# Moving one batch's v casts from GpSimd to VectorE, and working that batch's q halves in a row

## The chip, the cores and the metric

The kernel runs on one core of a Trainium2 chip. The metric is the device time of one execution in microseconds (us). A core has five engines with a queue each, worked in order: TensorE (PE in the profile, its weight loads PEld), VectorE (DVE), ScalarE (ACT), GpSimd (POOL) and SyncE (SP), which here only issues DMA transfers. Engines wait for each other through semaphores.

## The reference

Eight batches of linear attention feed a feed-forward layer with a "snake" activation:

```python
q_s = exp(q - max(q)) / sum(exp(q - max(q)))      # over the head dimension
k_s = exp(k - max(k)) / sum(exp(k - max(k)))      # over the sequence
kv  = einsum('bhsd,bhse->bhde', k_s, v)
a   = einsum('bhsd,bhde->bhse', q_s, kv)          # batch, heads, 576 rows, 64
x   = a.transpose(0, 2, 1, 3).reshape(4608, 512)
h   = x @ w_in                                    # 512 -> 2048
g   = h + sin(alpha * h)**2 / (alpha + 1e-9)
out = g @ w_out                                   # 2048 -> 512
```

q, k and v are float32 of shape (8, 8, 576, 64). The matmuls run in bfloat16.

## The kernel before

The 4608 rows are cut into nine tiles of 512. For a tile t, TensorE makes 16 blocks `hp` of 128 x 512 (four matmuls each). ScalarE takes the sine, one of three engines the square, VectorE combines `hp` and the square into `g`, and the second layer's matmuls (`op`) of tile t run under tile t + 1. A batch has 576 rows, so attention for the next batch is worked inside the tiles: batch 3 in tile 2. For it the kernel needs, on the way into tile 2, `qn` (q, exponential taken, divided by its sum, in two halves) and `vb` (v cast to bfloat16).

```python
def cast_v(b, engs):
    vv = vb[b % 2].rearrange("p j (i c) -> p i j c", i=4)
    for ii in range(2):                              # two casts of 128 x 1152
        engs[ii](vv[:, 2 * ii:2 * ii + 2, :, 0:D], staged["v", b][:, ii::2])

def norm_q(b, engs, j1=J, between=None):
    ...
    for ii in range(2):                              # two multiplies of 128 x 1152
        part = qs[:, 0:j1, 2 * ii:2 * ii + 2]
        if ii == 1 and between:
            between()
        ...
        engs[ii % len(engs)].tensor_tensor(qn[:, ii, 0:j1]..., qe[:, ii], part..., op=ALU.mult)
```

The head of tile 2, with cuts:

```python
kv_norm(2)
norm_q(3, [GP], between=lambda: cast_v(3, [GP_CP, GP_CP]))
take(os, 20)                                  # output matmuls of tile 1
...                                           # attention output of batch 2 into xT: tile 2's input
take(os)
q_transpose_dma(3)                            # on SyncE, waits for both halves of qn
load_batch(4)                                 # behind it in SyncE's queue
...
SQ2 = "PAPPAPAPPAPAPPAP"                      # who squares: P GpSimd, A ScalarE
for ni in range(nN):
    h_slot(2, ni, SQ2[ni], lag, lent)         # hp block, sine, square
    flush(lag, 2)                             # combine, two blocks behind
    attn_back(3, ni - 5, (DVE_CP, ACT_CP), (5, 7, 9, 10))
```

`attn_back` puts batch 3's key-value matmuls (`kvp`, 36 small ones) behind hp block 5, and its four output pairs (`xp`, one PSUM buffer) behind blocks 10, 12, 14 and 15. PSUM is the memory that TensorE accumulates into; from `kvp` VectorE makes `kbd`, which the `xp` matmuls take. There are four `hp` buffers in PSUM, plus two lent ones for blocks 4, 5, 10 and 11 (they bear the name `op` in the profile), and four `s` tiles for the sines. So block 6 can't start until combine 0 has freed a buffer.

The softmax here doesn't subtract the row's maximum and nothing guards it: scores larger than these inputs give would overflow.

## Time and profile before

| | before |
|---|---|
| median time (range, the first three runs) | 290.53 us (290.14 to 291.12) |
| profiled span | 288.3 us |
| TensorE busy, granted clock | 272.6 us (95%), 1.00 |
| GpSimd busy | 81.9 us (28%) |
| TensorE idle from 80 to 100 us | 2.75 us |

The page draws each engine's busy time in 40 slices of 7.2 us, a digit being tenths, 9 meaning 90% or more. TensorE's row of the kernel before:

```profile
PE   2899999999978999999999999999999999999994
```

Between the start and the end, the only digits under 9 are the 7 and the 8 in slices 12 and 13, at 79 to 94 us. This is tile 2's head, and the rest of the reading of before is in the prediction below.

### The profile page before, as it was taken

How to read it: one execution, taken by the hardware profiler on the slowest of the kernel's cores; microseconds unless marked ns; L12 is line 12 of the kernel's file. 1: busy time of each engine (PE TensorE's matmuls, PEld its weight loads, DVE VectorE, ACT ScalarE, POOL GpSimd, SP SyncE). 2: the span in 40 equal slices, each digit the busy share in tenths (PEclk: the TensorE clock that was granted, in tenths of full speed). 3: DMA queues.
4: the chain of work that ended last, by engine and by line, in shares of the span. 5: the costliest groups of instructions: out<-in, count | busy, mean ns of one | idle time of the engine just before them, and what ended most of it. 6: DMA issues, size and time to landing. Idle time of an engine off the chain costs nothing.

```text
span 288.3 us, 4247 instructions
## 1 busy us (share of the span) xinstructions
PE 272.6 (95%) x1541; PEld 130.7 (45%) x1569; DVE 189.4 (66%) x289; ACT 225.9 (78%) x321; POOL 81.9 (28%) x77
## 2 busy tenths in 40 slices
PE   2899999999978999999999999999999999999994
PEld 1444454445444445444544454445444444444443
DVE  4867967999839567856776677757674555555422
ACT  4898648999449999899889988999877777777400
POOL 2969502772486662005300440032000000000000
PEclk9999999999999999999999999999999999999999
DMA  7999999843959957119911990115011111111242
GB/s 263 305 201 243 258 399 407 298 163 89 273 121 374 411 208 140 38 38 356 291 24 24 330 343 3 38 39 132 22 39 36 36 36 39 36 38 38 46 101 73
DMA packets 38581, 45.77 MB, mean 159 GB/s; under 512 B 16528, under 2 KB 22432, under 8 KB 38560
## 3 DMA queue, kind: packets, MB, share of 16 engines
q1 hardware_dynamic: 33376, 40.57, 45.0%
q0 software_dynamic: 4992, 4.79, 9.6%
q8 instruction: 12, 0.20, 0.3%
q10 hardware_dynamic: 192, 0.14, 0.2%
q14 instruction: 9, 0.07, 0.1%
HBM read 36.71 MB, written 9.44 MB: 160 GB/s over the span
## 4 chain that ended last, share of the span: by engine, by line
PE 78%; DVE 6%; DMA 5%; POOL 4%; ACT 4%; issue 2%; ACTq 0%
PE op L270 37%; PE hp L250 33%; DMA st_v<-in_v_dram 3%; ACT s L256 3%; POOL s L260 2%; DVE g L266 2%; PE kvp L173 2%; PE xp L222 2%; DMA st_q<-in_q_dram 1%; PE op L590 1%; PE hh L250 1%; DVE qn L154 1%; DVE qs L152 1%; POOL vb L137 1%; POOL qn L154 1%
## 5 line engine op out<-in xcount | busy, mean ns | idle before, releaser
L266 DVE SCALAR_TENSOR_TENSOR g<-s,inva_sb,hp 128x512 bf16<-128x512 f32 x130 | 96.1, 745 | 64.2 <-ACT s L258 54.2
L250 PE MATMUL hp<-xT,win 128*128 128x512 bf16 x512 | 128.9, 379 | 2.3 <-DVE g L266 1.7
L270 PE MATMUL op<-wout,g 128*128 128x512 bf16 x479 | 121.8, 379 | 1.2 <-issue 0.6
L256 ACT ACTIVATE s<-hp,alpha_sb 128x512 f32<-128x512 f32 x130 | 87.9, 683 | 25.1 <-PE hp L250 22.6
L250 PEld LDWEIGHTS <-win 128*128 128x128 bf16 x576 | 56.3, 98 | 69.6 <-issue 3.0
L270 PEld LDWEIGHTS <-g 128*128 128x128 bf16 x560 | 54.1, 98 | 61.1 <-issue 0.4
L258 ACT ACTIVATE s<-s 128x512 f32<-128x512 f32 x111 | 69.9, 630 | 3.6
L154 POOL TENSOR_TENSOR qn<-qe,qs 128x1152 bf16<-128x1152 bf16 (+1 forms) x12 | 24.9, 2093 | 78.7 <-DVE qs L146 69.4
L260 POOL TENSOR_TENSOR s<-s 128x512 f32<-128x512 f32 x30 | 32.0, 1079 | 22.5 <-ACT s L256 22.2
L276 DVE COPY o<-op 128x512 f32<-128x512 f32 (+2 forms) x33 | 22.1, 669 | 9.7 <-PE op L270 5.8
L118 ACT ACTIVATE ke<-st_k 128x1152 bf16<-128x1152 f32 x16 | 17.9, 1151 | 5.1 <-DMA st_k<-in_k_dram 5.1
L118 ACT ACTIVATE qe<-st_q 128x1152 bf16<-128x1152 f32 (+3 forms) x18 | 17.6, 1024 | 2.1 <-DMA st_q<-in_q_dram 1.9
L145 DVE TENSOR_REDUCE qs<-qe 128x36 f32<-128x2304 bf16 x5 | 12.8, 2553 | 8.7 <-ACT qe L118 8.6
L137 POOL CAST vb<-st_v 128x1152 bf16<-128x1152 f32 x12 | 13.6, 1164 | 7.6 <-DMA st_v<-in_v_dram 6.4
L270 PE MATMUL hp<-wout,g 128*128 128x512 bf16 x62 | 14.8, 379 | 0.2 <-issue 0.2
L225 DVE CAST xT<-xp 128x512 bf16<-128x512 f32 (+1 forms) x18 | 13.4, 743 | 0.0
L173 PE MATMUL kvp<-vb,ke 64*128 64x130 bf16 x288 | 9.9, 216 | 0.8 <-ACT vb L137 0.4
L173 PEld LDWEIGHTS <-ke 64*128 64x128 bf16 x288 | 8.4, 93 | 5.0 <-issue 2.5
L118 ACT ACT_TABLE_LOAD x7 | 9.0, 1283 | 1.3 <-PEq L604 1.2
L250 PE MATMUL hh<-xT,win 128*128 128x512 bf16 x39 | 9.6, 379 | 0.1
L222 PE MATMUL xp<-qT,kbd 128*128 128x256 bf16 (+1 forms) x40 | 8.2, 286 | 0.8 <-DVE xT L225 0.8
L152 DVE TENSOR_REDUCE qs<-qe 128x16 f32<-128x1024 bf16 (+2 forms) x6 | 7.2, 1198 | 1.9 <-ACT qe L118 1.9
(79 smaller groups left out, 119.5 us busy)
## 6 DMA issues: line engine op xcount, KB each, us to landing
out_dram<-o SPq DMA_DIRECT2D x70, 128.0 KB, 2.3
st_q<-in_q_dram SPq DMA_DIRECT2D x6, 1152.0 KB, 5.9
st_k<-in_k_dram SPq DMA_DIRECT2D x6, 1152.0 KB, 8.2
st_v<-in_v_dram SPq DMA_DIRECT2D x6, 1152.0 KB, 10.1
st_k<-in_k_dram SPq DMA_DIRECT2D x4, 576.0 KB, 7.1
wout<-in_moe_w_out_dram POOLq DMA_DIRECT2D x4, 512.0 KB, 11.7
st_v<-in_v_dram SPq DMA_DIRECT2D x3, 576.0 KB, 9.4
win<-in_moe_w_in_dram POOLq DMA_DIRECT2D x6, 256.0 KB, 7.6
```

What stands on the lines that cost most here:

```text
L118: nc.scalar.activation(dst[:, :, ii * 128:(ii + 1) * 128].rearrange("p j (x d) -> p x j d", x=2), src[:, ii::2], AX.Exp)
L137: engs[ii](vv[:, 2 * ii:2 * ii + 2, :, 0:D], staged["v", b][:, ii::2])
L154: engs[ii % len(engs)].tensor_tensor(qn[:, ii, 0:j1].rearrange("p j (x d) -> p j x d", x=2), qe[:, ii], part.unsqueeze(3).to_broadcast([12 ...
L173: nc.tensor.matmul(kvp[:, e, ii * 130:(ii + 1) * 130], ke[r, j, ii * 128:(ii + 1) * 128], vt[r, j, ii * 130:(ii + 1) * 130], start=(j == 0 ...
L222: nc.tensor.matmul(xp[:, e, 0:n], kt[:, e, ii], qT[:, ii, j0:j1, e * 64:(e + 1) * 64], start=True, stop=True)
L250: nc.tensor.matmul(hp, win[:, ki, ni * 128:(ni + 1) * 128], xT[:, ki, t * MF:(t + 1) * MF], start=(ki == 0), stop=(ki == 3))
L256: nc.scalar.activation(s, hp, AX.Sin, scale=alpha_sb[:, ni:ni + 1])
L258: nc.scalar.activation(s, s, AX.Square)
L260: nc.gpsimd.tensor_tensor(s, s, s, op=ALU.mult)
L266: nc.vector.scalar_tensor_tensor(G[t][:, ni], in0=s, scalar=inva_sb[:, ni:ni + 1], in1=hp, op0=ALU.mult, op1=ALU.add)
L270: nc.tensor.matmul(acc, G[t][:, ni, j * 128:(j + 1) * 128], wout[:, ni, :], start=(ni == 0), stop=(ni == nN - 1))
L276: eng(o[:, cols], acc)
```

## The change

Its intent is to take GpSimd's two casts of v, and their wait for the load of v, out of the way of the second half of q and of tile 2's first squares.

```diff
-    def norm_q(b, engs, j1=J, between=None):
+    def norm_q(b, engs, j1=J):
...
-            if ii == 1 and between:
-                between()
...
-    norm_q(3, [GP], between=lambda: cast_v(3, [GP_CP, GP_CP]))
+    norm_q(3, [GP])
     take(os, 20)
...
     take(os)
+    cast_v(3, [DVE_CP, DVE_CP])
     q_transpose_dma(3)
     load_batch(4)
```

## The prediction

> **What bounds the kernel now.** I read the page first, then the chain that ended last between 60 and 100 us, then the timelines of TensorE, GpSimd, VectorE, ScalarE and SyncE there, then the table of busy time in stretches of 10 us.
>
> ```profile
> PE 272.6 (95%) x1541; PEld 130.7 (45%) x1569; DVE 189.4 (66%) x289; ACT 225.9 (78%) x321; POOL 81.9 (28%) x77
> ```
>
> TensorE is busy for 272.6 of 288.3 us at a granted clock of 1.00 throughout. A change that touches no matmul can gain only idle TensorE time. The table shows 1.91 us of it in 80 to 90 us and 0.84 in 90 to 100, against 0.05 to 0.21 in the steady stretches behind. That is the head of tile 2, where the changed lines run. The chain there:
>
> ```profile
> 76.61 1.74 PE hp L250 x8
> 78.35 0.07 issue
> 78.42 2.26 POOL vb L137 x2
> 80.68 2.09 POOL qn L154
> 82.77 1.01 POOL s L260
> 83.78 0.03 issue
> 83.80 2.74 DVE g L266 x4
> ```
>
> Columns: start, duration, work. For 5.4 us (78.42 to 83.78) the chain is on GpSimd: two casts of batch 3's v, the second half of batch 3's q, then the first square of tile 2. GpSimd's timeline shows why:
>
> ```profile
> 75.04 2.13 POOL L154 TENSOR_TENSOR qn<-qe,qs 128x1152 bf16<-128x1152 bf16 x1 [6.04 <-DVE qs L146]
> 78.42 2.26 POOL L137 CAST vb<-st_v 128x1152 bf16<-128x1152 f32 x2 [1.25 <-PE hp L250]
> 80.64 2.13 POOL L154 TENSOR_TENSOR qn<-qe,qs 128x1152 bf16<-128x1152 bf16 x1
> 82.73 3.04 POOL L260 TENSOR_TENSOR s<-s 128x512 f32<-128x512 f32 x3
> ```
>
> The 1.25 us is put down to a matmul, but a cast of v doesn't depend on hp. The load of v was issued at 71.85 and the DMA view gives it 6.4 us to land, so it landed at about 78.3: the wait is for that load. Squares back to back (3.04 us for three) show a backlog. The other engines meanwhile:
>
> ```profile
> 77.25 0.68 DVE L276 COPY o<-op 128x512 f32<-128x512 f32 x1
> 83.80 2.74 DVE L266 SCALAR_TENSOR_TENSOR g<-s,inva_sb,hp 128x512 bf16<-128x512 f32 x4 [5.87 <-POOL s L260]
> 84.64 0.69 ACT L256 ACTIVATE s<-op,alpha_sb 128x512 f32<-128x512 f32 x1 [3.77 <-DVE g L266]
> ```
>
> VectorE idles 5.87 us for the square; ScalarE idles 3.77 us, since only four s tiles exist and the first is freed by the first combine. TensorE stops later:
>
> ```profile
> 81.72 1.20 PE L173 MATMUL kvp<-vb,ke 64*128 64x130 bf16 x36
> 84.60 3.61 PE L250 MATMUL hp<-xT,win 128*128 128x512 bf16 x15 [1.69 <-DVE g L266]
> 88.39 1.02 PE L250 MATMUL op<-xT,win 128*128 128x512 bf16 x4 [0.17 <-DVE g L266]
> 91.94 0.43 PE L222 MATMUL xp<-qT,kbd 128*128 128x320 bf16 x2 [0.59 <-DVE xT L225]
> 95.38 0.43 PE L222 MATMUL xp<-qT,kbd 128*128 128x320 bf16 x2 [0.20 <-DVE xT L225]
> ```
>
> It had six accumulators filled ahead and batch 3's key-value matmuls to do, so 5.4 us of GpSimd chain cost it only 1.69 us directly, plus 0.17 + 0.59 + 0.20 = 0.96 us in the backlog. **The sum, 2.65 us, is the ceiling** of what this change can reach.
>
> **What the Trainium skill says.** "SBUF — State Buffer", section "Who interferes with whom": VectorE and GpSimd share a pair of SBUF ports under an exclusive lock; a VectorE instruction with two SBUF inputs, or a cast in a two-port mode, and a GpSimd instruction that reads SBUF wait for each other in full. "VectorE: DVE Perf Modes", section "Mode 2×_2P — use both read ports for one tensor": a single-source op from SBUF to SBUF on fp32 can take that mode at two results a cycle. The trace of before agrees on both as far as it goes:
>
> ```profile
> 34.90 1.70 POOL L154 TENSOR_TENSOR qn<-qe,qs 128x896 bf16<-128x896 bf16 x1 [3.23 <-DVE qs L153]
> 35.98 1.56 DVE L154 TENSOR_TENSOR qn<-qe,qs 128x896 bf16<-128x896 bf16 x1
> 42.33 0.76 DVE L137 CAST vb<-st_v 128x1152 bf16<-128x1152 f32 x1 [0.35 <-DMA st_v<-in_v_dram]
> ```
>
> VectorE's multiply of 1024 elements took 1.23 us with GpSimd idle, so 896 should take about 1.07; beside GpSimd it took 1.56, about what waiting to 36.60 and then running would give (1.69). The cast at 42.33 ran with GpSimd idle: 1152 elements in 0.76 us is 1.5 a ns, twice the multiply's 0.8, so it is in a two-results mode. That such a cast waits for GpSimd no row of before shows; I take it from the skill. "GPSIMD Engine Reference", section "Key points", calls VectorE about 2x faster at elementwise work; here the cast is 1.16 against 0.76 us, 1.5x.
>
> **The change part by part.**
>
> *Removed from GpSimd:* two casts (2.26 us) and their wait for the load (1.25 us, 77.17 to 78.42). The halves of q run in a row: 75.04 to 77.13, then to about 79.2 instead of 82.73, 3.5 us earlier.
>
> *Added to VectorE:* two casts of 0.76 us, 1.5 us. VectorE is free from 77.93 and the load lands at 78.4. By the lock, the first cast waits for GpSimd's q to end at 79.2. Then two casts (1.5) and the first square (1.04) share the port pair in some order. Casts first: 79.2 to 80.7, square to 81.7. Alternating: cast to 79.95, square to 81.0, cast to 81.75. Either way the first combine starts near 81.75 instead of 83.80. Without any lock it would be 80.35 (square 79.25 to 80.30).
>
> *What TensorE sees:* the key-value matmuls want the casts at 81.72: met within 0.1 us. They end at 82.9. The next hp block needs the first combine: 81.75 + 0.7 = 82.45, so the **1.69 us wait is gone**, with 0.4 us to spare (1.8 without a lock). I then walked the slots on with rows of this trace: sine 0.68 start to sine end, the square 0.72 behind the sine on ScalarE, 1.04 a square on GpSimd, 0.66 to 0.7 a combine, 0.86 an hp block.
>
> - hp 6, 7, 8, 9 start at 82.9, 83.7, 84.6, 85.4; combines 0 to 3 end at 82.4, 83.1, 83.8, 84.5: no wait. kbd (1.06 us) ends at 85.5.
> - hp 10 at 86.3 needs combine 4 (after kbd, 85.55 to 86.2): no wait, so the 0.17 goes too. The first xp pair takes 0.22, hp 11 and 12 end at 89.1.
> - The second xp pair needs VectorE's xT copy behind combine 8, which waits for GpSimd's squares 7 and 8: sine 7 ends at 86.2, square 8 at 88.2, combine 8 at 88.9, copy at 89.55. So xp starts at 89.6 instead of 91.94 (**2.3 us earlier**), with a wait of some 0.5 us where before has 0.59.
> - The last wait, 0.20, hangs on a square and a copy likewise; I leave it.
>
> Sum: 1.69 + 0.17 + about 0.1 of the 0.59, and also 0.3 to 0.4 that I can't assign: the start of the second xp pair says 2.3, the waits removed say 2.0. I take **2.2 us**.
>
> *Moved:* the transpose of q 3 waits for the second half of q in SyncE's queue, and batch 4's loads stand behind it:
>
> ```profile
> 82.80 1.78 SPq L212 DMA_TRANSPOSE qT<-qn  x1
> ```
>
> It moves to about 79.3, just behind the output writes (72.53 to 79.07), and the loads move with it. They were not waited for: ScalarE's exponential of q 4 at 97.96 follows its table load without idle. So no gain, and no harm if all of it moves by the same 2 to 3 us. The staging buffer of v 3, freed by the cast at about 81.7 instead of 80.7, is wanted by a load issued at 87.24 now, some 3.4 us earlier then: still later.
>
> *Behind tile 2:* to the end TensorE is full and the chain lies on it (steady idle 0.05 to 0.21 per 10 us). ScalarE's exponentials of batch 4 start when its last work of tile 2 ends, which follows the last hp block, so ScalarE moves with TensorE and the gain is carried to the end. 290.53 - 2.2 = **288.3 us**.
>
> **The rivals.**
>
> *The port lock eats it.* If the squares were starved or the casts took the port behind two squares, the casts would end at 82 to 83.3 and the key-value matmuls, in order on TensorE, would wait for them by up to 1.5 us; the gain falls to 0.5 to 1 us: 289.7. For it: qn and the squares read SBUF in exactly this stretch. Against: VectorE waits on the pair from 78.42, before the square is ready, and in the trace waits have been one instruction long.
>
> *GpSimd's squares become the bound.* Tile 2 gives GpSimd 10 squares of 16, 10.4 us, against 16 x 0.86 = 13.8 us of hp. That speaks against; but the 2-deep lag and the single xp buffer make them bite once or twice (the 0.59). If they gave back all but the first wait: gain 1.69, 288.8.
>
> *The casts are free and all goes:* the full 2.65, 287.9.
>
> *ScalarE's exponentials hold the end of the shift:* between 103.6 and 113.9 ScalarE has no idle and TensorE waits 0.2 us at 105.6. If batch 4's loads or ScalarE didn't follow, tile 3 would give back up to 1 us: 289.3.
>
> **Range and chances.** The rivals span 287.9 to 289.7 and the three runs of before lie 1.0 us apart. I put 8 in 10 on 287.6 to 289.4. Faster by over 2% needs 5.8 us, over twice the ceiling; slower by over 2% would need a new stall of that size, and no engine here has one in sight.
>
> **What would show it.** Right: the two q halves on GpSimd back to back from 75.0, the first square before 81, the first combine before 82, no TensorE wait before the hp block that follows the key-value matmuls, ScalarE's 3.77 us idle down to 1.5 or less, at least one cast on VectorE clearly over 0.76 us for the lock, and every later TensorE row some 2.2 us earlier. Wrong: a wait of the key-value matmuls for vb; the load of v landing after 79; casts at 0.76 us beside GpSimd (then the lock step is wrong, though not the total); or TensorE idle beyond 100 us that grows.

## The result, and the profile after

The time fell from a median of 290.93 us (290.14 to 292.12, five runs of the kernel before) to 287.85 us (287.56 to 288.01, five runs). The ratio is 0.9891, with a 95% interval of 0.9864 to 0.9918. Two repeats on other chips gave 0.9906 (0.9876 to 0.9936) and 0.9927 (0.9914 to 0.9941). The gain is thus 0.7 to 1.1%, and by the spans of the first two profiles 288.3 - 285.8 = 2.5 us. The larger ratios may hold a second effect: beside the first repeat, two of eleven executions of before took 292.2 us at a mean clock of 0.991 and 0.994, the other nine at most 291.2 us at 0.998 or more. Those two were not traced, so where their clock fell is not known.

The page after, engine totals and TensorE's slices:

```profile
PE 272.6 (95%) x1541; PEld 130.8 (46%) x1569; DVE 192.6 (67%) x291; ACT 226.0 (79%) x321; POOL 80.6 (28%) x75
...
PE   2899999999999999999999999999999999999994
```

TensorE does the same 272.6 us of work and its 7 and 8 are gone. VectorE has two instructions more, GpSimd two fewer. VectorE's busy time rose by 3.2 us although two casts should cost 1.5; the experiments show why. GpSimd's timeline at the head of tile 2 (start, duration, engine, line, work; line numbers are two lower than before):

```profile
75.02 4.21 POOL L152 TENSOR_TENSOR qn<-qe,qs 128x1152 bf16<-128x1152 bf16 x2 [6.04 <-DVE qs L146]
79.19 4.07 POOL L258 TENSOR_TENSOR s<-s 128x512 f32<-128x512 f32 x3
```

The halves of q run in a row and the first square is dispatched at 79.19 instead of 82.73. Three squares take 4.07 us where they took 3.04. VectorE and ScalarE:

```profile
78.11 3.25 DVE L137 CAST vb<-st_v 128x1152 bf16<-128x1152 f32 x2 [0.20 <-DMA st_v<-in_v_dram]
81.28 2.75 DVE L264 SCALAR_TENSOR_TENSOR g<-s,inva_sb,hp 128x512 bf16<-128x512 f32 x4
82.11 0.69 ACT L254 ACTIVATE s<-op,alpha_sb 128x512 f32<-128x512 f32 x1 [1.25 <-DVE g L264]
```

The wait in front of the cast names the load of v, as the prediction had read the mislabelled wait of before. The first combine starts at 81.28 instead of 83.80, and ScalarE's wait for a free s tile is 1.25 instead of 3.77 us. TensorE:

```profile
81.70 1.20 PE L171 MATMUL kvp<-vb,ke 64*128 64x130 bf16 x36
82.83 3.63 PE L248 MATMUL hp<-xT,win 128*128 128x512 bf16 x15
86.30 1.03 PE L248 MATMUL op<-xT,win 128*128 128x512 bf16 x4
...
89.40 0.43 PE L220 MATMUL xp<-qT,kbd 128*128 128x320 bf16 x2
...
92.92 0.43 PE L220 MATMUL xp<-qT,kbd 128*128 128x320 bf16 x2 [0.28 <-DVE xT L223]
```

Of the four waits of before (1.69, 0.17, 0.59, 0.20) the profile shows one, of 0.28 us. The chain that ended last, between 60 and 100 us, no longer holds GpSimd's casts and q:

```profile
71.84 6.25 DMA st_v<-in_v_dram
78.08 0.02 issue
78.11 3.25 DVE vb L137 x2
81.36 2.67 DVE g L264 x4
```

Now the load of v and the casts on VectorE set the combines. This chain says which instruction released which, and not that TensorE loses time to it: TensorE has no wait before the hp block at 82.83.

SyncE's transpose of q 3 came earlier as well, with batch 4's loads behind it:

```profile
79.26 1.87 SPq L210 DMA_TRANSPOSE qT<-qn  x1
```

It was at 82.80. That leaves several possible causes of the 2.5 us, which the runs below tell apart.

### The profile page after: what moved, and what is told of

Read it like the earlier page. It is cut to its first block, busy times and chain, and to the rows that moved or that the text cites. A ratio compares the mean times of both kernels' runs of the same rounds, so it can differ in the third digit from the quotient of the medians.

```text
span 285.8 us, 4247 instructions
## 1 busy us (share of the span) xinstructions
PE 272.6 (95%) x1541; PEld 130.8 (46%) x1569; DVE 192.6 (67%) x291; ACT 226.0 (79%) x321; POOL 80.6 (28%) x75
## 4 chain that ended last, share of the span: by engine, by line
PE 74%; DVE 9%; DMA 7%; ACT 4%; issue 3%; POOL 2%; SPq 0%; ACTq 0%
PE op L268 33%; PE hp L248 33%; DMA st_v<-in_v_dram 5%; ACT s L254 3%; DVE g L264 2%; POOL s L258 2%; PE kvp L171 2%; DVE qs L150 2%; PE xp L220 2%; DMA st_q<-in_q_dram 1%; PE op L589 1%; PE hh L248 1%; DVE vb L137 1%; DVE qn L152 1%; DVE kbd L184 1%
## 5 line engine op out<-in xcount | busy, mean ns | idle before, releaser
L258 POOL TENSOR_TENSOR s<-s 128x512 f32<-128x512 f32 x30 | 33.0, 1111 | 22.3 <-ACT s L254 22.0
L137 POOL CAST vb<-st_v 128x1152 bf16<-128x1152 f32 x10 | 11.3, 1163 | 6.5 <-DMA st_v<-in_v_dram 6.5
```

The source lines that it names most:

```text
L258: nc.gpsimd.tensor_tensor(s, s, s, op=ALU.mult)
```

## The experiments

Theory 1 is the prediction's: TensorE loses time only because GpSimd's first square of tile 2, and so the first combine, comes later than the accumulators last. Rival 2: the gain is the faster cast on VectorE. Rival 3: the gain is the earlier transpose and earlier loads.

Profiled executions start up to 2.4 us apart, so each row of this table counts from the start of tile 2's first hp block (76.44 in the kernel before). "Block 6" is the hp block behind the key-value matmuls, "tile 3" is tile 3's fifth hp block, whose start takes in everything that tile 2 gained or lost.

The column "tile 3" is, for example, 105.78 - 76.44 = 29.34 in the kernel before and 103.23 - 76.43 = 26.80 in the changed one.

| kernel | first square | first combine | block 6 | tile 3 | tile 3 against before | ratio of times |
|---|---|---|---|---|---|---|
| before | 6.29 | 7.36 | 8.16 | 29.34 | | 1 |
| changed | 2.76 | 4.85 | 6.40 | 26.80 | -2.54 | 0.9891 |
| e1, q in a row, GpSimd casts | 4.98 | 6.05 | 6.85 | 28.02 | -1.32 | 0.9964 |
| e3, three extra multiplies | 6.91 | 7.99 | 8.79 | 30.83 | +1.49 | 1.0061 |
| e8, two extra multiplies | 5.78 | 6.85 | 7.65 | 28.82 | -0.52 | 0.9998 |
| e4, one-port casts | 2.76 | 4.63 | 6.41 | 26.79 | -2.55 | 0.9910 |
| e5, no casts | 2.76 | 3.83 | 6.41 | 26.79 | -2.55 | 0.9919 |
| e7, ScalarE casts | 4.66 | 5.73 | 6.53 | 28.41 | -0.93 | 0.9974 |

From tile 3's fifth block to the end of the span, all of these take 182.5 to 183.0 us. What tile 2 gains or loses is carried to the end, within 0.5 us. The two longest, e8 and e7, wait 0.39 and 0.43 us at about 175 us (start to start, as explained below) for a DMA transpose of q; the others do not.

### The changed kernel again

> The changed kernel again, on the chip of the runs beside it. Expected as before: about 2.5 us under the kernel before (ratio 0.989 to 0.993), profile span near 285.8 us.

> The changed kernel once more, to stand beside the two runs below on one chip: ratio 0.989 to 0.993 to before.

Measured: 288.12 us and ratio 0.9906; 288.22 us and 0.9927. Both ratios were as expected; the first profile's span was 286.7 us, not 285.8, as it began 0.9 us late. All of e1 to e3 ran beside the first, e8 and e9 beside the second, e4 to e7 on a third chip.

### e1: half of the change

```diff
-    norm_q(3, [GP])
+    norm_q(3, [GP])
+    cast_v(3, [GP_CP, GP_CP])
...
-    cast_v(3, [DVE_CP, DVE_CP])
```

> Half of the change: both halves of q in a row on GpSimd, and then the casts, still on GpSimd (2.26 us). Theory 1 (TensorE loses only because the first square of tile 2 comes late on GpSimd, by more than its accumulators last): q 75.0 to 79.2, casts to 81.45 without a wait for the load, first square at 81.45 instead of 82.73 (before) or 79.2 (after), the hp block behind the key-value matmuls at about 83.3 with a wait of about 0.4 us (1.69 before, 0 after). Everything 1.3 us earlier than before: about 1.3 us of the 2.5 us, ratio near 0.9955. Rival 2 (the gain is the cast on the faster engine, VectorE instead of GpSimd): nothing is gained, ratio 1.000. Rival 3 (the gain is the earlier transpose and earlier loads of batch 4 in SyncE's queue, which move to 79.3 here just as in the whole change): all of the 2.5 us, ratio 0.9915.

Measured: 289.61 us, ratio 0.9964 (0.9930 to 0.9999). This profiled execution began 2.38 us late (its granted clock was 0.66 from 15 to 20 us), so 2.38 is to be taken off its times. GpSimd and TensorE in its timeline:

```profile
81.57 2.27 POOL L137 CAST vb<-st_v 128x1152 bf16<-128x1152 f32 x2
83.80 3.04 POOL L258 TENSOR_TENSOR s<-s 128x512 f32<-128x512 f32 x3
...
85.67 3.61 PE L248 MATMUL hp<-xT,win 128*128 128x512 bf16 x15 [0.38 <-DVE g L264]
```

The first square came 1.3 us earlier than before (4.98 against 6.29), TensorE's wait fell from 1.69 to 0.38, and tile 3 started 1.32 us earlier. Rival 2 expected nothing and rival 3 all of it. Theory 1 said 1.3. The interval of the ratio only just leaves out both rivals; it is the trace that tells them apart. About half of the change's gain needs no other engine at all: it is the wait for the load of v, which the second half of q no longer sits through, while the casts behind it find v already there.

### e2: the casts on VectorE in the old place

```diff
-    norm_q(3, [GP], between=lambda: cast_v(3, [GP_CP, GP_CP]))
+    norm_q(3, [GP], between=lambda: cast_v(3, [DVE_CP, DVE_CP]))
```

> The casts on VectorE, but emitted where GpSimd's casts stood, so that on VectorE they stand ahead of the output copies and the xT copies of tile 2. GpSimd works both halves of q in a row here too. Theory 1 with in-order queues: VectorE waits at 74.8 for the load of v until 78.1, and then for GpSimd's q until 79.1, casts to 80.6, and only then 2.6 us of copies that tile 2 starts from: first hp block at about 83.2 instead of 76.43, TensorE idle 6 to 7 us, time about 6.5 us over the changed kernel, about 294.5 us, slower than before by 1.4% (ratio near 1.014). Rival 2 (only the engine of the cast matters, not its place): as fast as the changed kernel, ratio 0.9915.

Measured: 294.4 us, ratio 1.0136 (1.0091 to 1.0180). VectorE and TensorE:

```profile
78.24 2.26 DVE L137 CAST vb<-st_v 128x1152 bf16<-128x1152 f32 x2 [3.46 <-DMA st_v<-in_v_dram]
...
81.74 5.02 PE L250 MATMUL hp<-xT,win 128*128 128x512 bf16 x14 [4.95 <-DVE xT L528]
```

VectorE waited 3.46 us for v with the copies that tile 2 starts from queued behind it. TensorE lost 4.95 us, less than the 6 to 7 expected, but then ran at a granted clock of 0.50 from 82 to 85 us, which cost some 1.6 us more. The total was right and its split was not. The place of the cast in VectorE's queue is as much a part of the change as the engine.

### e3 and e8: squares late, everything else as changed

```diff
     norm_q(3, [GP])
+    flat78 = q78.rearrange("p i j d -> p (i j d)")     # no longer read
+    for _ in range(3):                                 # e8: range(2)
+        nc.gpsimd.tensor_tensor(flat78, flat78, flat78, op=ALU.mult)
     take(os, 20)
```

> The changed kernel with three extra multiplies of 128 by 512 on GpSimd (on a tile that is no longer read) behind the second half of q and ahead of tile 2's squares. The transpose and the loads of batch 4 stay early, as in the changed kernel, and the casts stay on VectorE; only the squares come late. Theory 1: extra multiplies and casts share the port pair, the first square starts at about 83.2 (before: 82.73), the hp block behind the key-value matmuls waits about 2.2 us, and the whole gain is gone: ratio 0.999 to 1.003 to before. Rival 2 (faster cast) and rival 3 (earlier loads): the gain of 2.5 us stays, ratio 0.9915.

Measured: 292.04 us, ratio 1.0061 (1.0018 to 1.0104). Casts stay on VectorE and the transpose stays early, and still the whole gain is gone, and more. So rivals 2 and 3 fall as causes of it. GpSimd, TensorE, and then one stretch of 3 us (stretch, its length, busy time of PE, PEld, DVE, ACT and POOL, then the granted clock, DMA share and GB/s):

```profile
79.41 4.19 POOL L522 TENSOR_TENSOR q<-q 128x512 f32<-128x512 f32 x3
83.55 3.04 POOL L258 TENSOR_TENSOR s<-s 128x512 f32<-128x512 f32 x3
...
85.43 5.30 PE L248 MATMUL hp<-xT,win 128*128 128x512 bf16 x15 [2.31 <-DVE g L264]
...
86.00:89.00 3.00, 3.00 (x9) 1.12 (x8) 2.92 (x7) 2.94 (x6) 1.63 (x2) 0.54 1.01 401
```

The late squares give a wait of 2.31 us, as expected. The surplus is the second number of that matmul row: 15 matmuls took 5.30 us instead of 3.61, because the granted clock fell after the wait, to 0.54 on average from 86 to 89 us. One execution was traced; all four had a mean clock of 0.988 to 0.994, which fits such a dip in each. I then took one multiply away to see the late squares without the dip:

> As the run with three extra multiplies on GpSimd, but with two. Three made TensorE wait 2.31 us, after which the granted clock of TensorE fell to 0.50 for some 3 us, and the time rose 1.3 us more than the late squares account for. With two, the squares start at about 82.3 and the wait is 1.2 to 1.4 us, less than the 1.69 us of before. If the late squares alone set the loss and the clock dip came on top: no dip in the profile, first hp block behind the key-value matmuls at about 84.1, 2.0 us over the changed kernel, ratio to before 0.997 to 0.999. If the extra loss with three had another cause that goes with the number of multiplies: over before here too, ratio above 1.001.

Measured: 290.20 us, ratio 0.9998 (0.9982 to 1.0014), with clock 1.00.

```profile
82.86 3.03 POOL L258 TENSOR_TENSOR s<-s 128x512 f32<-128x512 f32 x3
...
84.73 3.61 PE L248 MATMUL hp<-xT,win 128*128 128x512 bf16 x16 [1.18 <-DVE g L264]
```

The wait is 1.18 us, the matmuls behind it take 3.61 us again, and tile 3 starts 0.52 us earlier than before, where the first square was 0.51 earlier. The ratio came out 0.001 above what was expected. In the trace 0.4 us is lost later on: the `xp` matmuls at 175.40 wait for a transposed q. The row shows 0.23 us of it; from start to start it is 175.40 - 175.01 = 0.39, so all of it in this execution. Between e1, e8 and before, 1.3 us of first square is worth 1.32 us and 0.51 us is worth 0.52: in this range TensorE pays one for one.

### e4: casts that don't take the second port

```diff
-    cast_v(3, [DVE_CP, DVE_CP])
+    def reduce_cp(dst, src):                           # a sum over one element
+        with nc.allow_low_precision(reason="a sum over one element"):
+            nc.vector.tensor_reduce(dst, src.unsqueeze(4), axis=AXL.X, op=ALU.add)
+    cast_v(3, [reduce_cp, reduce_cp])
```

> The changed kernel, but each cast is written as a sum over one element, so that it is a reduction: one SBUF input,[...] which by the Trainium skill never takes the port pair that VectorE shares with GpSimd. Lock theory: each takes 1.25 to 1.35 us (1152 elements of a reduction took 1.30 us elsewhere), the first starts when v has landed at 78.1 and does not wait for q on GpSimd, both end at about 80.8 (81.36 in the changed kernel although each needs only 0.76 us there), the first three squares on GpSimd take 3.04 us instead of 4.07, the first combine starts at about 80.8. Rival without a lock (the casts were slow for another reason, such as the load's own writes or memory bandwidth): squares stay at 4.07 us or the reductions are stretched as well, to over 1.5 us each. Time in either case within 0.3 us of the changed kernel, for TensorE has no wait there.

What this takes from the Trainium skill stands in "SBUF — State Buffer", section "Who interferes with whom".

Measured: 287.74 us, ratio 0.9910 (0.9897 to 0.9923), the result correct. VectorE and GpSimd:

```profile
78.61 2.62 DVE L536 TENSOR_REDUCE vb<-st_v 128x1152 bf16<-128x1152 f32 x2 [0.62 <-DMA st_v<-in_v_dram]
...
79.27 3.21 POOL L258 TENSOR_TENSOR s<-s 128x512 f32<-128x512 f32 x3
```

This settles the port lock. In the changed kernel the two casts took 1.74 and 1.59 us although one alone took 0.76, and two of the three squares 1.55 instead of 1.04. A reduction takes 1.36 and 1.35 us, at little over half a cast's rate, and waits for nobody (the first ran from 78.61 beside GpSimd's q, which ended at 79.31), and the squares beside it take the 3.21 us that they take with no cast at all (e5). Slower by itself, it is quicker here: 2.62 us for both against 3.25. The time is that of the changed kernel, as expected, since TensorE has slack there.

### e5: no casts at all

```diff
-    cast_v(3, [DVE_CP, DVE_CP])
```

> The changed kernel with the casts of batch 3's v left out (a wrong result on purpose: batch 1's v stands in). Theory 1: after the change the casts cost next to nothing, since TensorE's wait behind the key-value matmuls is already zero: the first combine starts at 80.3 and time falls by 0 to 0.3 us against the changed kernel. If the lock or the casts on VectorE still cost TensorE time, it falls by more than 0.5 us. The result is expected to be wrong.

Measured: 287.93 us, ratio 0.9919 (0.9903 to 0.9934), and a wrong result. VectorE:

```profile
80.36 2.92 DVE L264 SCALAR_TENSOR_TENSOR g<-s,inva_sb,hp 128x512 bf16<-128x512 f32 x4 [2.35 <-POOL s L258]
```

The first combine starts 1.0 us earlier than with casts and TensorE gains nothing (26.79 against 26.80 at tile 3). The casts, with the lock, are wholly hidden.

### e7: the casts on ScalarE

```diff
-    cast_v(3, [DVE_CP, DVE_CP])
+    cast_v(3, [ACT_CP, ACT_CP])
```

> The changed kernel with both casts on ScalarE at the same place, ahead of tile 2's sines. Theory 1: ScalarE waits for v until 78.1 and casts for 2.3 us, so the first sine ends at about 81.1 instead of 78.2, the first square runs from 81.1 to 82.1, the first combine from 82.2, the hp block behind the key-value matmuls waits 0.1 to 0.3 us, and ScalarE's backlog makes the later waits somewhat longer: 0.3 to 1 us over the changed kernel, ratio 0.993 to 0.996 to before. Rival 2 (only VectorE is the right engine): no gain or a loss against before.

Measured: 289.50 us, ratio 0.9974 (0.9959 to 0.9988). ScalarE and TensorE (0.43 us to be taken off):

```profile
78.63 2.23 ACT L137 CAST vb<-st_v 128x1152 bf16<-128x1152 f32 x2 [3.74 <-DMA st_v<-in_v_dram]
...
87.99 1.02 PE L248 MATMUL op<-xT,win 128*128 128x512 bf16 x4 [0.77 <-DVE g L264]
```

It gains about a third (0.93 of 2.54 us at tile 3), less than I expected. Block 6 was met with 0.1 us of wait, as worked out, but the backlog cost much more than I allowed: 0.77 us before block 10 and two waits of 0.31 and 0.47 for xp. ScalarE holds the sines that every square waits for, so 2.2 us there delays all of them, while VectorE stands behind the squares.

### e6 and e9: an attempt to go on

```diff
-        attn_back(3, ni - 5, (DVE_CP, ACT_CP), (5, 7, 9, 10))
+        attn_back(3, ni - 5, (DVE_CP, ACT_CP), (4, 6, 8, 10))
...                                                          # e9 only:
-            want = 23 + 21 * ni // 8 if b is not None else 4 * (ni + 1)
+            want = (26 if t == 3 else 23) + 21 * ni // 8 if b is not None else 4 * (ni + 1)
```

> The changed kernel with the four batch-3 output pairs of tile 2 at blocks 9, 11, 13 and 15 instead of 10, 12, 14 and 15, so that two hp blocks stand between them and the single xp buffer has time to be emptied. The one TensorE wait left in tile 2 is 0.28 us, ahead of the last pair. Expected: that wait gone, the second pair may wait up to 0.2 us instead; time 0 to 0.3 us under the changed kernel, which is at the edge of what the times resolve, so read from the trace.

Measured: 287.88 us, ratio 0.9925 (0.9903 to 0.9947). The wait before the last xp pair is gone, and TensorE in tile 3 shows a new one:

```profile
103.65 1.02 PE L248 MATMUL hp<-xT,win 128*128 128x512 bf16 x4 [0.61 <-DVE g L264]
```

Tile 3's fifth block waits for its first combine, which waits for the first sine, which stands behind ScalarE's exponentials of batch 4.

> The run with xp pairs at blocks 9, 11, 13 and 15 took away the last wait of tile 2 (0.28 us), but tile 3 then waited 0.61 us for its first combine, which hangs on ScalarE's exponentials of batch 4. Here three more output matmuls (0.216 us each, 0.65 us) of tile 2 go before tile 3's second hp block, to fill that wait. If that wait was what took the gain back: it is 0 to 0.1 us, and the time is 0.3 to 0.7 us under the changed kernel on the same chip (ratio to before lower by 0.001 to 0.002, at the edge of what the times resolve). If ScalarE holds the whole tile: the wait only moves to a later hp block and nothing is gained.

Measured: 288.10 us, ratio 0.9930 (0.9917 to 0.9942), beside the changed kernel's 288.22 us and 0.9927.

```profile
104.20 0.38 PE L268 MATMUL op<-wout,g 128*128 128x512 bf16 x1 [0.78 <-DVE o L274]
```

The wait moved: now an output matmul waits for an output copy that stands behind the same late combine on VectorE. Counted from tile 2's first hp block to the end, e6 and e9 take 209.4 and 209.7 us, the changed kernel 209.3. No version here beats it. At tile 3's head ScalarE is the next limit: there TensorE already waits 0.20 us in the kernel before and 0.12 in the changed one (start to start).

## Why the prediction was right, point by point

- **The total.** 288.3 us was predicted, 287.85 measured, inside 287.6 to 289.4, and within 2% as foreseen. By the spans the gain is 2.5 us, where 2.2 was predicted.
- **GpSimd's late first square is the cause.** Shown by e1, e3 and e8: the square's time moves and TensorE follows, and in e3 and e8 the casts' engine, the transpose and the loads are as in the changed kernel. That the cast's own speed on VectorE doesn't matter is shown by e4 and e5: whether the casts take 3.25 us, 2.62 or none, the time is the same.
- **The first combine near 81.75.** It started at 81.28. Casts and squares alternated, one instruction at a time. The estimate summed whole records, while the locked instructions overlap by about 0.1 us at each hand-over.
- **No wait for vb, no wait at block 6, none at block 10.** All three hold: 82.83, against 82.9 worked out, and 86.30 against 86.3.
- **The second xp pair at 89.6, and "0.3 to 0.4 that I can't assign".** It started at 89.40. The unassigned part is a mis-sized term: the profile's idle in front of TensorE rows is too short. Matmuls follow each other every 0.216 us, yet each record is 0.38 long, so an end that is followed by a wait is drawn 0.16 us late. Behind the small key-value matmuls the error is 0.06. Counting from start to start, at 0.216 us a matmul, gives for the four waits:

| wait of TensorE, start to start | before | after |
|---|---|---|
| hp block 6 | 84.60 - 82.85 = 1.75 | 0.00 |
| hp block 10 | 88.39 - 88.06 = 0.33 | 0.01 |
| second xp pair | 91.94 - 91.19 = 0.75 | 89.40 - 89.10 = 0.30 |
| fourth xp pair | 95.38 - 95.02 = 0.36 | 92.92 - 92.48 = 0.44 |
| sum | 3.19 | 0.75 |

  The gain is 2.44 us. With 0.09 more before tile 3's fifth block it is the 2.5 us of the spans. So "the sum, 2.65 us, is the ceiling" was low by half a microsecond; by the rows it was 3.19, plus the 0.2 in tile 3.
- **The last wait, left as it was.** It grew slightly, from 0.36 to 0.44.
- **The lock rival.** The lock that the prediction took from "SBUF — State Buffer" is there (e4), but it costs TensorE nothing (e5): the first combine still ends before block 6 wants its buffer. One reading behind it was loose: while VectorE's multiply of 1024 elements took 1.23 us, GpSimd was not idle but issuing DMA transfers (6.03 to 11.39 us). The total doesn't rest on it.
- **The squares rival.** GpSimd's squares still hold up the second and fourth xp pairs, but gave back nothing of the first two waits. That is also why not all of the idle goes: 0.75 of 3.19 us stays.
- **The ScalarE rival.** It gave nothing back, but e6 and e9 show it as the next limit. The prediction put that risk at up to 1 us; the wait there is 0.12 us, less than the 0.20 of before.
- **The expectations of the runs** missed five times: the split of the loss in e2, the size of e3 (the clock), of e7 (ScalarE's backlog) and, by 0.001, of e8 (a later wait), and the 0 to 0.3 us hoped for in e6. Of the two outcomes named for e9 the second came.

## What to carry to other kernels

Ask of a helper engine not how busy it is but what stands in its queue in front of the first thing the main engine will want: GpSimd was 28% busy and cost 2.5 us, because two casts and their wait for a load sat ahead of the second half of q and the first square. Half of the gain came from the order alone, and the move to another engine was right only at a place in its queue where its input had landed and nothing urgent stood behind. Size TensorE's idle from start to start, and check in the next stretch which engine will be met when TensorE comes earlier.

## What the Trainium skill lacked or had wrong

- **"SBUF — State Buffer", "Who interferes with whom":** it holds for the cast (0.76 us alone, 1.74 and 1.59 us beside GpSimd's multiplies) and for reductions (no wait, 1.36 and 1.35 us). It says that whoever issues first gets the ports; what it lacks is the order that follows when both engines have work queued: here they took turns, one instruction each. It also doesn't say that the blocked time is drawn as busy: VectorE's busy time rose by 3.2 us for 1.5 us of work.
- **"TensorE: Matmul & The Clock Gate", "Why this matters for your kernels":** it warns of idle gaps over about 3 us. In the one trace of e3 the clock fell behind a wait of 2.31 us (2.38 from start to start): 0.54 from 86 to 89 us, 1.7 us lost. Waits of 1.18 us (e8) and 1.69 us (before) left it at 1.00 in the profiled executions; of two untraced executions of before with a mean clock of 0.991 and 0.994 it is not known. Whether the small key-value matmuls ahead of the wait count towards it was not tested.
- **"Perfetto Trace Analysis", "Tensor Engine Instruction (MATMUL, LD_WEIGHTS)":** it says that a matmul's end is estimated. It doesn't say what follows for waits: with records of 0.38 us at a spacing of 0.216 us, a wait is shown 0.16 us too short (0.06 behind the small key-value matmuls), here 0.54 us over four waits.
